# A load moved to another queue, two weight transfers cut into four, and some products moved ahead of scores, in a fused gated-attention and bilinear feed-forward kernel

## The chip, the cores and the metric

The kernel runs on one core of one Trainium2 chip. Its engines work side by side, each through its own list of instructions in order: TensorE (PE; its weight loads are shown as PEld), VectorE (DVE), ScalarE (ACT), GpSimd (POOL) and SyncE (SP). The metric is the device time of one launch in microseconds; less is better. A time is the median of several runs. The profile is that of one further execution.

## The reference

Four batches, eight heads, 768 positions, 48 numbers per head. A gated recurrence gives y, and y, with heads side by side (384 columns, 3072 tokens), goes through a bilinear feed-forward block.

```python
for t in range(S):
    state = alpha[:, :, t, :, None] * state + einsum('bhd,bhe->bhde', k[:, :, t], v[:, :, t])
    y[:, :, t] = einsum('bhd,bhde->bhe', q[:, :, t], state)
x = y.transpose(0, 2, 1, 3).reshape(B * S, H * D)
out = (x @ w_a) * (x @ w_b) @ w_out      # w_a, w_b: 384 x 1536, w_out: 1536 x 384
```

## The kernel before

**Chunks.** The work is cut into six chunks, 0 to 5, each of two batches (its halves u = 0 and 1) and 256 positions, two positions on each of 128 partitions. Chunks 0 and 1 hold the first 256 positions, 2 and 3 the next, 4 and 5 the last; the state goes on from 0 to 2 to 4 and from 1 to 3 to 5.

**The attention part of a chunk.** Alphas are loaded (a_t) and their logs taken on ScalarE (L420). Pairs of logs are added (L428; in later chunks L433 and L436, three instructions) and split into terms of lower precision (L474 and L482, or L497 twice), and TensorE sums them along the positions with a triangular matrix (L512 or L507). Exponentials of the sums (L541) scale keys and queries into QKp (L552); a query is first multiplied with a ratio (L519, L526), a key with an alpha (L526). QKp is turned into kqT: by TensorE and a copy (L593, L599, L601) in chunks 0 and 1, by a transposing DMA on SyncE's queue (L604) in chunks 2 to 5. Scores are products of kqT (L674), masked and moved out of PSUM by VectorE (L679) or by ScalarE and then VectorE (L683, L687). y is summed in PSUM from the carried state (L698, L703) and from scores and values (L698, L724). The copy of y out of PSUM (L764, L766) is xT in chunks 0 and 1; in later chunks it is ys, and a transposing DMA on SyncE's queue (L771) makes xT of it. The state is updated from L627 by L659 to L663.

**The feed-forward part.** The 1536 columns are 12 slices of 128. A product a or b of a slice is three matmuls (L786) over 256 tokens (one half of a chunk) or 512 (both). ScalarE moves a out of PSUM (L792, tiles as_, three buffers), VectorE multiplies it with b into prod (L800). When all 12 are there, an output of 128 tokens is 12 matmuls (L808), in two halves of six; it is moved out (L823, L825) and stored (L841). PSUM has eight banks of 512 columns; a bank can be written again when its reader is done.

**The order** is written out by hand, in a text called PROGRAM: each word is one operation, the number ahead of a line is the chunk, and the last letter of many names the engine (V, P for GpSimd, S, Y for SyncE). The text is run from top to bottom, so each engine's list is in the order of the text. Words that matter here: `ld` load, `W` a load of weight columns, `ln` the logs, `lx` or `l2` pair sums, `R`, `H` and `L` the splits, `A2`, `AQ` the sums, `ra` the ratio, `lv` the multiply with ratio or alpha, `mk`, `mq` the scaling into QKp, `T` the transposing DMA of QKp, `D` scores, `M`, `Mc`, `Mm` masking, `SA`, `SB`, `Y` the parts of y, `X` its copy and `XT` its transposing DMA, `K`, `KA`, `k` the state, `a f u i`, `b f u i` products of slice f into bank i (`*` for both halves), `as` and `pr` their way out, `o m h i` half h of output m, `ot`, `st` its way out. `gate...` is a copy of a single element on GpSimd: GpSimd goes on only when that element is written.

**The queues.** A load on GpSimd occupies that engine for 0.75 to 1.2 us while it is issued, and its queue serves one transfer behind the other. The weights, cast from float32 to bfloat16 on the way, come through GpSimd's queue, as do values, Wo and the loads of chunks 0 to 3 for the most part. SyncE's queue carries loads of later chunks, stores and the transposing DMAs, issued in the order of the text; each waits for its data before the next is issued. The alphas' tile a_t has two buffers, the tiles of logs and pair sums one.

In PROGRAM the load of chunk 4's alphas (`4: ld a * P`) stands among chunk 2's multiplies, ahead of `T 1` and `T 0` of chunk 2; that of chunk 5's (`5: ld a * Y`) stands behind chunk 2's `XT 0`.

Of the kernel before, what the change touches and what calls it, by code (L numbers as in the profile page):

```python
# [20 lines left out]
0: cm 1; ld v 1 P; c2 P; c3 P; D 0 1 5; M 0 1; D 0 0 0; SB 0 6; B 1a 4; Bs 1a; Mc 0 0; Mm 0 0 V; B 1b 5; Bs 1b; E 1a i; E 1a b; mq 1a V; mk 1a V; K 0 1 4; E 1b i  # L21
0: v 1 V; mk 1b V; E 1b b; mq 1b V; SA 0; Y 0; X 0 S; dk 1 0; C 1 0 3; Ce 1 0 V; k 0 1 V; b 1 0 6; W a 0 256; de 1; K 1 0 5; k 1 0 V
1: ld a 1 P
0: W a 256 768; W b 256 768
1: ld a 0 P
0: W a 768 1536; C 1 1 1; a 1 0 2; as 1 0; pr 1 0; Ce 1 1 V; W b 768 1536
1: ld q 0 P; ln 1
0: b 0 0 4; a 0 0 2; as 0 0; pr 0 0; D 1 0 6; D 1 1 0; M 1 1
1: ld k 0 P; l2 1 P; ld v 0 P; ld k 1 P
0: Mc 1 0; Mm 1 0 V  # L30
1: H 1 S
0: SB 1 1; a 2 0 3; a 5 0 6; a 3 0 7; as 3 0; a 4 0 4; as 4 0; as 5 0; b 4 0 0; b 3 0 7
1: L 1 V
0: pr 4 0; pr 3 0; SA 1; Y 1; X 1 V; b 2 0 0
1: A2 1 7; ld q 1 P
0: Wo 0 6
2: ld a * P
0: K 1 1 5
1: ln 0
0: as 2 0; pr 2 0  # L40
1: l2 0 V; E 1 b; E 1 i; H 0 S
0: a 3 1 4; a 5 1 2; k 1 1 V; as 3 1; b 3 1 0; a 4 1 1; b 5 0 7; pr 5 0; as 5 1; a 6 * 5; b 5 1 4; a 11 * 3; pr 5 1; pr 3 1; as 4 1; b 4 1 1; pr 4 1
1: L 0 V; dk * 6
0: Wo 6 12; as 11 *; as 6 *
1: ra 0
0: b 6 * 3; pr 6 *; b 11 * 0; pr 11 *
# [1 line left out]
1: lv 0 q P  # L48
2: ld q * P
1: ld v 1 P; lv 0 k V; mk 0 V  # L50
0: a 10 * 2; a 7 * 3
1: E 0 b; mq 0 V
0: as 10 *; a 2 1 4; as 2 1; b 10 * 1; pr 10 *; as 7 *; b 7 * 0; pr 7 *
1: v 0 S; ra 1
0: b 2 1 3; a 0 1 5
1: C 0 0 4
0: a 1 1 6; as 1 1
1: Ce 0 0 S
0: pr 2 1; b 1 1 1; pr 1 1; as 0 1
1: KA 0 02; k 0 0 V; k 0 1 V; C 0 1 7  # L60
0: b 0 1 6
1: Ce 0 1 S
2: ld k * P
1: lv 1 k P
0: pr 0 1
1: mk 1 V; lv 1 q P; mq 1 V
3: ld a * P
0: a 8 * 1; as 8 *; a 9 * 5; as 9 *
2: ld v * P
0: b 8 * 2; pr 8 *  # L70
1: D 0 0 6; M 0 0; D 0 1 3; Mc 0 1; SB 0 4
# [21 lines left out]
1: a 7 0 3; b 11 0 1; pr 11 0; KA 1 64; k 1 0 V; k 1 1 V; b 10 0 5; a 10 0 7; as 10 0; a 0 0 6  # L93
2: lv 0 k V
1: pr 10 0; b 0 0 1; a 3 0 4; as 0 0; pr 0 0
2: lv 1 k P; mk 1 V
1: as 3 0; b 3 0 7; a 1 0 6; as 1 0
4: ld a * P
1: b 7 0 0; b 1 0 4; pr 1 0; as 7 0; pr 7 0; pr 3 0
2: mk 0 V  # L100
1: SB 1 0
3: ln *
1: a 6 0 2; as 6 0; b 9 0 3; a 4 0 5; a 9 0 6; as 9 0; pr 9 0
2: mq 1 V; T 1
0: o 2 0 4
1: b 4 0 6; b 6 0 7
2: lv 0 q P; mq 0 V
1: pr 6 0
2: T 0
3: ld k * Y  # L110
# [15 lines left out]
1: pr 6 1  # L126
3: R 0
2: Mm 1 0 V
1: o 2 0 7
2: SB 1 3; D 0 1 1; Mc 0 1; Mm 0 1 V; k * 1 V  # L130
3: R 1
1: o 2 1 -; ot 2 S
0: st 2 Y
1: st 2 Y
2: D 0 0 5; Mc 0 0; Mm 0 0 V; gatem 0 0; SB 0 1; SA 1; Y 1; X 1 S; XT 1
3: lv 0 k P; lv 1 k P
1: a 4 1 7
4: ln *
1: as 4 1; b 9 1 0; pr 9 1; o 0 0 5
3: AQ 3  # L140
2: SA 0; Y 0; X 0 S; XT 0
5: ld a * Y
1: o 0 1 -; ot 0 V; a 1 1 6; a 10 1 1; as 1 1; as 10 1
3: E 0 b; E 0 i
1: b 4 1 2; pr 4 1; b 8 1 5; b 1 1 1; a 8 1 6; b 10 1 0; pr 1 1; o 3 0 2; pr 10 1; as 8 1; pr 8 1; o 3 1 -; ot 3 S; st 3 Y
2: a 4 * 7; as 4 *
3: E 1 b
2: a 5 * 6; b 4 * 3
3: E 1 i
1: st 0 Y  # L150
3: dr
4: lx V; R 0
3: mk 0 V; mq 0 V; T 0
4: ld q * Y
2: a 1 * 2; b 5 * 0; as 5 *; pr 5 *
4: ra 1
2: b 7 * 4; b 10 * 1; pr 4 *; a 10 * 6; as 10 *; pr 10 *
3: mk 1 V
2: a 7 * 0; b 1 * 5; a 0 * 6; b 0 * 7; as 1 *; as 7 *; pr 1 *; pr 7 *; as 0 *; a 3 * 0; b 9 * 1; pr 0 *
3: mq 1 V  # L160
# [5 lines left out]
3: KA * 06; D 0 0 4; M 0 0; dl; k * 0 V; k * 1 V  # L166
1: o 1 0 2
2: b 11 * 7
5: ln *
2: a 11 * 5; as 11 *; pr 11 *  # L170
1: o 1 1 -; ot 1 S
2: a 6 * 5; as 6 *; a 8 * 3; as 8 *
3: SB 0 6; D 0 1 0; M 0 1; T 1
4: ld k * Y
3: D 1 0 4; Mc 1 0
2: b 6 * 2; pr 6 *; b 8 * 3; pr 8 *
4: R 1
# [93 lines left out]
def kernel(  # L271
# [29 lines left out]
    ld = ctx.enter_context(tc.tile_pool(name="ld", bufs=2))  # L301
# [668 lines left out]
```

## Time and profile before

| | us |
|---|---|
| timed runs | 194.47, 194.94, 197.66 |
| median | 194.94 |
| profiled execution | 193.93 |
| its span, first to last instruction | 192.2 |
| granted TensorE clock | 0.999 |

A line of a group or timeline reads: start, duration, engine, line of the kernel, operation, what is written <- what is read, shapes, the number of instructions (x), and in brackets the idle time of that engine just before and what ended it. In the list of DMA issues the last number is the median time from issue to landing. A matmul's duration has a tail that runs beside the next one, so the cost of a further matmul is taken from the starts of two lines or from the chain. SyncE's lines (SPq) are the issuing of DMAs, not their transfer.

The DMA engines are busy from the start to about 115 us, and then in bursts (share of the 16 engines in 40 slices of the span, in tenths: 6999999999999999949993586998196005031013).

### The profile page before, as it was taken

The numbers are of one execution on the slowest core, as the hardware profiler recorded it, in microseconds if no ns is written. First come the engines' busy times: TensorE is split into PE (matmuls) and PEld (weight loads), VectorE is DVE, ScalarE is ACT, GpSimd is POOL, SyncE is SP. The second block draws the span as 40 slices with busy tenths as digits, with TensorE's granted clock in tenths as the row PEclk, the third lists the DMA queues.
The fourth block names the chain that finished last, engine by engine and source line by source line (L and its number), as shares of the span: only waits on it lengthen the run. The fifth ranks groups of instructions, "written<-read, shape, count | busy, mean of one in ns | idle before, by whom it ended". The sixth has DMA issues, their size and how long they took to land.

```text
span 192.2 us, 5878 instructions
## 1 busy us (share of the span) xinstructions
PE 184.1 (96%) x2509; PEld 111.3 (58%) x2509; DVE 136.1 (71%) x230; ACT 103.1 (54%) x189; POOL 50.1 (26%) x72
## 2 busy tenths in 40 slices
PE   7979799999999998999999999999999999999993
PEld 3567576766777875644556644555544565544562
DVE  4778767999899796688979499864953961156520
ACT  4385566887585567446566135875266521164301
POOL 8999746920641404000400020050000000000000
PEclk9999999999999999999999999999999999999999
DMA  6999999999999999949993586998196005031013
GB/s 149 246 216 215 243 241 254 249 245 261 252 233 219 191 213 248 215 126 229 151 220 54 141 185 154 160 173 111 47 198 144 3 3 123 3 108 56 2 41 123
DMA packets 67162, 30.96 MB, mean 161 GB/s; under 512 B 58064, under 2 KB 65120, under 8 KB 67136
## 3 DMA queue, kind: packets, MB, share of 16 engines
q0 software_dynamic: 18640, 14.16, 41.9%
q1 hardware_dynamic: 48352, 16.34, 40.6%
q8 instruction: 19, 0.31, 0.7%
q10 hardware_dynamic: 144, 0.10, 0.2%
q14 instruction: 7, 0.06, 0.1%
HBM read 25.98 MB, written 4.74 MB: 160 GB/s over the span
## 4 chain that ended last, share of the span: by engine, by line
PE 86%; POOL 6%; DMA 4%; issue 1%; DVE 0%; ACT 0%; POOLq 0%; DVEq 0%
PE psum L786 48%; PE psum L808 24%; DMA wb_t<-in_moe_w_b_dram 4%; PE psum L674 3%; PE psum L724 2%; PE psum L627 2%; PE psum L698 2%; PE psum L703 1%; PE psum L507 1%; PE psum L819 1%; POOL v_t L413 1%; PE psum L593 1%; POOL a_t L413 1%; POOL wa_t L393 1%; POOL k_t L413 0%
## 5 line engine op out<-in xcount | busy, mean ns | idle before, releaser
L786 PE MATMUL psum<-xT,wb_t 128*128 128x512 bf16 (+1 forms) x270 | 57.0, 337 | 0.6 <-DMA wb_t<-in_moe_w_b_dram 0.5
L786 PE MATMUL psum<-xT,wa_t 128*128 128x512 bf16 (+1 forms) x270 | 56.1, 337 | 1.1 <-issue 0.7
L808 PE MATMUL psum<-wo_t,prod 128*128 128x384 bf16 x276 | 48.5, 326 | 0.0
L786 PEld LDWEIGHTS <-wb_t 128*128 128x128 bf16 x270 | 25.5, 98 | 21.1 <-DMA wb_t<-in_moe_w_b_dram 0.8
L786 PEld LDWEIGHTS <-wa_t 128*128 128x128 bf16 x270 | 25.6, 98 | 20.8 <-issue 1.0
L808 PEld LDWEIGHTS <-prod 128*128 128x128 bf16 x276 | 26.1, 98 | 16.9
L683 ACT ACTIVATE m<-psum 128x1024 bf16<-128x1024 f32 x16 | 16.3, 1023 | 6.5 <-PE psum L674 6.3
L825 DVE COPY ot<-psum 128x384 f32<-128x384 f32 (+1 forms) x13 | 6.9, 539 | 15.9 <-PE psum L808 13.4
L526 POOL TENSOR_TENSOR q_t<-q_t,ra 128x384 f32<-128x384 f32 x8 | 8.7, 1084 | 34.3 <-DMA q_t<-in_q_dram 17.3
L823 ACT ACTIVATE ot<-psum 128x384 f32<-128x384 f32 (+1 forms) x12 | 5.7, 477 | 12.9 <-PE psum L808 11.9
L420 ACT ACTIVATE la<-a_t 128x1536 f32<-128x1536 f32 (+2 forms) x9 | 9.5, 1057 | 3.4 <-DMA a_t<-in_alpha_dram 3.4
L687 DVE TENSOR_TENSOR m<-m,mask 128x1024 bf16<-128x1024 bf16 x16 | 10.8, 685 | 0.3 <-ACT m L683 0.3
L679 DVE TENSOR_TENSOR m<-psum,mask 128x1024 bf16<-128x1024 f32 x8 | 9.8, 1222 | 1.7 <-PE psum L674 1.5
L526 POOL TENSOR_TENSOR k_t<-k_t,a_t 128x384 f32<-128x384 f32 x5 | 5.3, 1064 | 19.0 <-DVE QKp L552 17.5
L552 DVE TENSOR_TENSOR QKp<-k_t,invb 128x768 bf16<-128x768 f32 x10 | 9.9, 992 | 0.2
L552 DVE TENSOR_TENSOR QKp<-q_t,beta 128x768 bf16<-128x768 f32 x10 | 9.3, 949 | 0.0
L674 PE MATMUL psum<-kqT 64*64 64x128 bf16 x384 | 8.6, 218 | 0.5 <-DVE prod L800 0.2
L413 POOL DMA_DIRECT2D v_t<-in_v_dram x8 | 8.6, 1070 | 0.5 <-issue 0.4
L674 PEld LDWEIGHTS <-kqT 64*64 64x64 bf16 x384 | 6.3, 107 | 3.2 <-issue 2.1
L764 ACT ACTIVATE ys<-psum 128x768 bf16<-128x768 f32 x7 | 5.6, 809 | 4.3 <-PE psum L703 2.3
L413 POOL DMA_DIRECT2D a_t<-in_alpha_dram x6 | 6.3, 1042 | 4.0 <-DMA wa_t<-in_moe_w_a_dram 2.2
L446 PE MATMUL psum<-wz 128*128 128x512 bf16 x17 | 5.5, 472 | 1.2 <-DVE og L338 1.2
(273 smaller groups left out, 270.9 us busy)
## 6 DMA issues: line engine op xcount, KB each, us to landing
out_dram<-ot SPq DMA_DIRECT2D x23, 192.0 KB, 2.2
a_t<-in_alpha_dram POOLq DMA_DIRECT2D x3, 768.0 KB, 14.5
k_t<-in_k_dram SPq DMA_DIRECT2D x3, 768.0 KB, 7.2
q_t<-in_q_dram POOLq DMA_DIRECT2D x2, 768.0 KB, 13.0
v_t<-in_v_dram POOLq DMA_DIRECT2D x4, 384.0 KB, 10.1
q_t<-in_q_dram SPq DMA_DIRECT2D x2, 768.0 KB, 6.6
a_t<-in_alpha_dram POOLq DMA_DIRECT2D x3, 384.0 KB, 5.6
q_t<-in_q_dram POOLq DMA_DIRECT2D x3, 384.0 KB, 13.4
```

What stands on the lines that cost most here:

```text
L413: eng.dma_start(out=t[:, us, hs].rearrange("p b h r d -> p (b h) (r d)"), in_=src[ch.b0 + us.start:ch.b0 + us.stop, hs, ch.s * 2 * C:(ch.s ...
L420: nc.scalar.activation(out=ch.la[:, us, hs].rearrange("p b h r d -> p (b h r d)"), in_=ch.a[:, us, hs].rearrange("p b h r d -> p (b h r d) ...
L526: eng.tensor_mul(x, x, by)
L552: eng.tensor_mul(QKp[ch.c % 2][:, u, j, :, hs, :D], src[:, u, hs].rearrange("p h r d -> p r h d"), f)
L674: nc.tensor.matmul(s2[g * HC:(g + 1) * HC, r, p, rk, :], lhsT=ch.kqT[u][rs, 1, rk, 2 * h + p, g * HC:(g + 1) * HC], rhs=queriesT(ch, u, 2 ...
L679: nc.vector.tensor_mul(m.rearrange("p r a k s -> p (r a) (k s)"), ch.s2[u, h].rearrange("p r a k s -> p (r a) (k s)"), maskn(4))
L683: nc.scalar.activation(out=m.rearrange("p r a k s -> p (r a) (k s)"), in_=ch.s2[u, h].rearrange("p r a k s -> p (r a) (k s)"), func=AF.Copy)
L687: eng.tensor_mul(x, x, maskn(4))
L786: nc.tensor.matmul(p, lhsT=(wa_t, wb_t)[w][:, kk, f * 128:(f + 1) * 128], rhs=ch.xT[:, us.start // 2:us.stop // 2, kk].rearrange("p u g s ...
L808: nc.tensor.matmul(op, lhsT=ch.prod[:, f, at:at + C], rhs=wo_t[:, f, :], start=(f == 0), stop=(f == NFF - 1))
L823: nc.scalar.activation(out=o_, in_=i_, func=AF.Copy)
L825: eng.tensor_copy(o_, i_)
```

## The change

Only PROGRAM and one new gate are changed.

- The weights' columns 256 to 768 come as four transfers instead of two: a 256 to 512, b 256 to 512, a 512 to 768, b 512 to 768. Six products of slices 2 to 5 for chunk 0's first half are put in that order, with those of a and b taking turns; b of slices 2 and 3 now stand ahead of chunk 0's second y. Some banks change.
- A product of both halves (`a 10 *`) stands ahead of `b 6 *`, and `a 1 1` of chunk 0 ahead of chunk 1's first turning (`C 0 0`).
- Chunk 4's alphas are loaded by SyncE behind chunk 2's `XT 0`, in the place of chunk 5's, and those by SyncE behind chunk 4's keys. Logs, pair sums and splits of both chunks move back with them: chunk 4's `ln` and a ratio behind ScalarE's eviction of chunk 2's second slice (`as 5 *`), its `lx` behind `pr 4 *`, its first split behind chunk 3's output half.
- In chunk 2, `mq 1` and `T 1` stand ahead of `mk 0`; a gate lets GpSimd multiply the other half's queries only when `mk 1` has written.
- `a 4 1` and the output half `o 0 0` of chunk 1 stand ahead of chunk 2's last scores (`D 0 0`), `o 0 1` ahead of chunk 2's last y (`Y 0`).

```diff
-0: W a 256 768; W b 256 768
+0: W a 256 512; W b 256 512; W a 512 768; W b 512 768
...
-0: SB 1 1; a 2 0 3; a 5 0 6; a 3 0 7; as 3 0; a 4 0 4; as 4 0; as 5 0; b 4 0 0; b 3 0 7
-1: L 1 V
-0: pr 4 0; pr 3 0; SA 1; Y 1; X 1 V; b 2 0 0
+0: a 2 0 4; as 2 0; a 3 0 5; as 3 0; b 2 0 6; pr 2 0; b 3 0 0; a 4 0 7; as 4 0; a 5 0 1; as 5 0; pr 3 0
+1: H 1 S; L 1 V
+0: SA 1; Y 1; X 1 V; b 4 0 4; pr 4 0; b 5 0 5; pr 5 0
...
-2: lv 1 k P; mk 1 V
+2: lv 1 k P; mk 1 V; gatek 1; lv 0 q P
 1: as 3 0; b 3 0 7; a 1 0 6; as 1 0
-4: ld a * P
 1: b 7 0 0; b 1 0 4; pr 1 0; as 7 0; pr 7 0; pr 3 0
-2: mk 0 V
+2: mq 1 V; T 1
...
-2: mq 1 V; T 1
+2: mk 0 V
...
-2: D 0 0 5; Mc 0 0; Mm 0 0 V; gatem 0 0; SB 0 1; SA 1; Y 1; X 1 S; XT 1
+1: a 4 1 5; as 4 1; o 0 0 7
+2: D 0 0 1; Mc 0 0; Mm 0 0 V; gatem 0 0; SB 0 5; SA 1; Y 1; X 1 S; XT 1
 3: lv 0 k P; lv 1 k P
-1: a 4 1 7
-4: ln *
-1: as 4 1; b 9 1 0; pr 9 1; o 0 0 5
+1: o 0 1 -; ot 0 V
 3: AQ 3
+1: b 9 1 0; pr 9 1
 2: SA 0; Y 0; X 0 S; XT 0
-5: ld a * Y
+4: ld a * Y
...
+    def gate_k(x, u):
+
+        nc.gpsimd.tensor_copy(go, QKp[x.c % 2][0:1, int(u), 1, 0, 0, 0:1])
```

More of the change, by code (lines that the diff above doesn't have):

```diff
@@ L27 @@
 1: ld q 0 P; ln 1
-0: b 0 0 4; a 0 0 2; as 0 0; pr 0 0; D 1 0 6; D 1 1 0; M 1 1
+0: b 0 0 4; a 0 0 2; as 0 0; pr 0 0; D 1 0 6; SB 1 2; D 1 1 0; M 1 1
 1: ld k 0 P; l2 1 P; ld v 0 P; ld k 1 P
 0: Mc 1 0; Mm 1 0 V
-1: H 1 S
-0: SB 1 1; a 2 0 3; a 5 0 6; a 3 0 7; as 3 0; a 4 0 4; as 4 0; as 5 0; b 4 0 0; b 3 0 7
-1: L 1 V
-0: pr 4 0; pr 3 0; SA 1; Y 1; X 1 V; b 2 0 0
+0: a 2 0 4; as 2 0; a 3 0 5; as 3 0; b 2 0 6; pr 2 0; b 3 0 0; a 4 0 7; as 4 0; a 5 0 1; as 5 0; pr 3 0
+1: H 1 S; L 1 V
+0: SA 1; Y 1; X 1 V; b 4 0 4; pr 4 0; b 5 0 5; pr 5 0
 1: A2 1 7; ld q 1 P
@@ L37 @@
 2: ld a * P
-0: K 1 1 5
+0: K 1 1 6
 1: ln 0
-0: as 2 0; pr 2 0
 1: l2 0 V; E 1 b; E 1 i; H 0 S
-0: a 3 1 4; a 5 1 2; k 1 1 V; as 3 1; b 3 1 0; a 4 1 1; b 5 0 7; pr 5 0; as 5 1; a 6 * 5; b 5 1 4; a 11 * 3; pr 5 1; pr 3 1; as 4 1; b 4 1 1; pr 4 1
-1: L 0 V; dk * 6
+0: a 3 1 1; a 5 1 2; k 1 1 V; as 3 1; b 3 1 0; a 4 1 3; as 5 1; b 5 1 4; as 4 1; b 4 1 5; pr 3 1; pr 5 1; a 6 * 6; a 11 * 7; pr 4 1
+1: L 0 V; dk * 1
+0: a 10 * 2
 0: Wo 6 12; as 11 *; as 6 *
@@ L50 @@
 1: ld v 1 P; lv 0 k V; mk 0 V
-0: a 10 * 2; a 7 * 3
+0: a 7 * 4
 1: E 0 b; mq 0 V
-0: as 10 *; a 2 1 4; as 2 1; b 10 * 1; pr 10 *; as 7 *; b 7 * 0; pr 7 *
+0: as 10 *; a 2 1 5; as 2 1; b 10 * 1; as 7 *; b 7 * 0; pr 7 *; pr 10 *
 1: v 0 S; ra 1
-0: b 2 1 3; a 0 1 5
-1: C 0 0 4
-0: a 1 1 6; as 1 1
+0: b 2 1 3; a 0 1 6; a 1 1 4
+1: C 0 0 5
+0: as 1 1
 1: Ce 0 0 S
-0: pr 2 1; b 1 1 1; pr 1 1; as 0 1
-1: KA 0 02; k 0 0 V; k 0 1 V; C 0 1 7
-0: b 0 1 6
+0: pr 2 1; b 1 1 7; pr 1 1; as 0 1
+1: KA 0 02; k 0 0 V; k 0 1 V; C 0 1 1
+0: b 0 1 4
 1: Ce 0 1 S
@@ L67 @@
 3: ld a * P
-0: a 8 * 1; as 8 *; a 9 * 5; as 9 *
+0: a 8 * 7; as 8 *; a 9 * 5; as 9 *
 2: ld v * P
@@ L103 @@
 1: a 6 0 2; as 6 0; b 9 0 3; a 4 0 5; a 9 0 6; as 9 0; pr 9 0
-2: mq 1 V; T 1
+2: mk 0 V
 0: o 2 0 4
 1: b 4 0 6; b 6 0 7
-2: lv 0 q P; mq 0 V
+2: mq 0 V
 1: pr 6 0
@@ L128 @@
 2: Mm 1 0 V
-1: o 2 0 7
+1: o 2 0 6
 2: SB 1 3; D 0 1 1; Mc 0 1; Mm 0 1 V; k * 1 V
@@ L134 @@
 1: st 2 Y
-2: D 0 0 5; Mc 0 0; Mm 0 0 V; gatem 0 0; SB 0 1; SA 1; Y 1; X 1 S; XT 1
+1: a 4 1 5; as 4 1; o 0 0 7
+2: D 0 0 1; Mc 0 0; Mm 0 0 V; gatem 0 0; SB 0 5; SA 1; Y 1; X 1 S; XT 1
 3: lv 0 k P; lv 1 k P
-1: a 4 1 7
-4: ln *
-1: as 4 1; b 9 1 0; pr 9 1; o 0 0 5
+1: o 0 1 -; ot 0 V
 3: AQ 3
+1: b 9 1 0; pr 9 1
 2: SA 0; Y 0; X 0 S; XT 0
-5: ld a * Y
-1: o 0 1 -; ot 0 V; a 1 1 6; a 10 1 1; as 1 1; as 10 1
+4: ld a * Y
+1: a 1 1 1; a 10 1 2; as 1 1; as 10 1
 3: E 0 b; E 0 i
-1: b 4 1 2; pr 4 1; b 8 1 5; b 1 1 1; a 8 1 6; b 10 1 0; pr 1 1; o 3 0 2; pr 10 1; as 8 1; pr 8 1; o 3 1 -; ot 3 S; st 3 Y
+1: b 4 1 7; pr 4 1; b 8 1 0; b 1 1 5; a 8 1 6; b 10 1 1; pr 1 1; o 3 0 2; pr 10 1; as 8 1; pr 8 1; o 3 1 -; ot 3 S; st 3 Y
 2: a 4 * 7; as 4 *
@@ L151 @@
 3: dr
-4: lx V; R 0
 3: mk 0 V; mq 0 V; T 0
@@ L155 @@
 2: a 1 * 2; b 5 * 0; as 5 *; pr 5 *
-4: ra 1
-2: b 7 * 4; b 10 * 1; pr 4 *; a 10 * 6; as 10 *; pr 10 *
+4: ln *; ra 1
+2: b 7 * 4; b 10 * 1; pr 4 *
+4: lx V
+2: a 10 * 6; as 10 *; pr 10 *
 3: mk 1 V
@@ L168 @@
 2: b 11 * 7
-5: ln *
 2: a 11 * 5; as 11 *; pr 11 *
@@ L172 @@
 2: a 6 * 5; as 6 *; a 8 * 3; as 8 *
+4: R 0
 3: SB 0 6; D 0 1 0; M 0 1; T 1
 4: ld k * Y
+5: ld a * Y
 3: D 1 0 4; Mc 1 0
@@ L196 @@
 4: mq 0 V; mk 0 V
-5: lx V
+5: ln *; lx V
 3: a 9 * 3; a 0 * 2; a 8 * 6; b 11 * 7; as 9 *; as 11 *; as 0 *; pr 11 *; b 9 * 2; b 0 * 1; pr 9 *
@@ L867 @@
         "gatet": gate_t,
+        "gatek": gate_k,
         "gatem": gate_m,
```

## The prediction

> **What bounds the kernel now.** I read the page first, then TensorE's waits, then the chain of waits in order of time, then each engine's timeline around the places where TensorE stands still. From the page, the span, the busy shares and the chain's shares:
>
> ```profile
> span 192.2 us, 5878 instructions
> PE 184.1 (96%) x2509; PEld 111.3 (58%) x2509; DVE 136.1 (71%) x230; ACT 103.1 (54%) x189; POOL 50.1 (26%) x72
> ...
> PE 86%; POOL 6%; DMA 4%; issue 1%; DVE 0%; ACT 0%; POOLq 0%; DVEq 0%
> ```
>
> TensorE is the bound: 86% of the chain. What a change of order can win is the time in which TensorE stands idle, and the chain shows where that is (start, us, what; an "issue" piece is idle time without a waiter):
>
> ```profile
> 14.42 8.19 DMA wb_t<-in_moe_w_b_dram
> ...
> 23.48 0.95 PE psum L698 x54
> ...
> 74.52 0.51 PE psum L724 x32
> ...
> 76.32 0.72 issue
> ...
> 79.30 1.95 PE psum L808 x12
> ```
>
> TensorE's own timeline has the rest, the wait for weights at 20 to 23 us; and its weight loads (PEld) have one wait at 66 us, which the list of waits puts on VectorE but which a transposing DMA ends:
>
> ```profile
> 20.67 1.48 PE L786 MATMUL psum<-xT,wa_t 128*128 128x256 bf16 x12 [0.39 <-DMA wa_t<-in_moe_w_a_dram]
> 22.65 0.83 PE L786 MATMUL psum<-xT,wb_t 128*128 128x256 bf16 x6 [0.50 <-DMA wb_t<-in_moe_w_b_dram]
> ...
> 25.51 0.83 PE L786 MATMUL psum<-xT,wa_t 128*128 128x256 bf16 x6
> ```
> ```profile
> 66.12 0.48 PEld L674 LDWEIGHTS <-kqT 64*64 64x64 bf16 x32 [0.50 <-DMA kqT<-QKp]
> ```
>
> After 23 us the idle time is thus 0.50 + 0.72 = 1.2 us of 192. Everything that follows is about single microseconds, against the 3.9 us that are 2%, about what a measurement of this kernel can tell from no change.
>
> **Part 1, the weights in four transfers.** Before, weight columns 256 to 768 come as two transfers of 384 KB, the first landing at 20.6, the second at 22.61. After, four of 192 KB. If a half costs half, they land near 19.5, 20.5, 21.6 and 22.6. Before, TensorE has only the four a-products of slices 2 to 5 to do until 22.65; b of 2, 3 and 4 and the second half of chunk 0's y (23.48, 0.95) follow. A product of three 256-column matmuls costs (1.48 - 0.83) / 2 = 0.33, from the rows with twelve and with six. After, b of 2 and 3 and that y run before the last quarter lands; only b of 4 and 5 wait for it. Step by step: b of 2 by 21.0 (its bank is free when ScalarE has read the scores), b of 3 at 21.4 (the bank is masked until then), a of 4 and 5 by 22.4, y by 23.35, b of 4 and 5 by 24.0, chunk 1's sums and state 24.0 to 24.7, then the products that start at 25.51 now, with b of slice 5 (0.33) already done: 25.51 - 24.75 + 0.33 = about 1.1 us in hand.
>
> That time does not reach the end. Chunk 1's first keys come through the same queue behind all weights, and VectorE's chain hangs on them:
>
> ```profile
> 32.61 0.56 DVE L526 TENSOR_TENSOR k_t<-k_t,a_t 128x384 f32<-128x384 f32 x1 [0.31 <-DMA k_t<-in_k_dram]
> ...
> 34.15 0.95 DVE L552 TENSOR_TENSOR QKp<-q_t,beta 128x768 bf16<-128x768 f32 x1
> ...
> 46.75 0.96 DVE L497 TENSOR_TENSOR ll<-lh 128x768 f32<-128x768 f32 x1
> ```
> ```profile
> 35.26 0.61 PE L593 MATMUL psum<-ident,QKp 128*128 128x128 bf16 x8
> 35.71 0.49 PE L786 MATMUL psum<-xT,wa_t 128*128 128x256 bf16 x3
> ...
> 47.88 0.36 PE L507 MATMUL psum<-l,utb 64*64 64x384 bf16 x4
> ```
>
> The multiply of the queries ends at 35.10 and TensorE turns them at 35.26. The changed order has put one more product (a of slice 1, the row at 35.71, 0.33) ahead of this turning; so at 35.2 the lead is 0.33 and at most 0.1 more, and the rest of the 1.1 goes into a wait. VectorE is then busy almost without a gap to 47.71, 0.17 before chunk 2's sums on TensorE. So this part is worth **0.35 us**, as long as the keys land at the same time.
>
> Do halves cost half? The nearest rows are issue times and issue-to-landing times of transfers that follow one another in that queue:
>
> ```profile
> 15.18 0.89 POOL L413 DMA_DIRECT2D a_t<-in_alpha_dram  x1
> ...
> 18.42 0.90 POOL L413 DMA_DIRECT2D k_t<-in_k_dram  x1
> ...
> 20.27 0.92 POOL L413 DMA_DIRECT2D v_t<-in_v_dram  x1
> ```
> ```profile
> a_t<-in_alpha_dram POOLq DMA_DIRECT2D x1, 384.0 KB, 8.7
> ```
> ```profile
> k_t<-in_k_dram POOLq DMA_DIRECT2D x1, 384.0 KB, 14.1
> ```
> ```profile
> v_t<-in_v_dram POOLq DMA_DIRECT2D x1, 192.0 KB, 13.2
> ```
>
> Two more issues hold GpSimd for at most 0.9 us each. The loads behind them don't feel it: they lie 8.7 to 14 us in the queue. A pair sum of chunk 1 behind them on GpSimd comes up to 1.8 us later; with its split on ScalarE and VectorE it reaches TensorE about when that asks for it, at 24.0. Were it 0.3 late, the wait for the keys would hide it.
>
> Alphas of 384 KB land at 23.9, 1.3 us behind the weights at 22.6; values of 192 KB land at 33.5, 1.0 behind the keys at 32.5. Read as a fixed part, that is 2 x 1.0 - 1.3 = 0.7 us in each transfer, and two more transfers would put the keys 1.4 us later. Read as the values' short rows (they are cast on the way), it says nothing of weights, whose rows stay long. At the other end, nothing is lost. I take 0, since the queue is never empty here and transfers overlap, and keep 1.4 for the range. The Trainium skill (DMA: Bandwidth & Descriptors, Rules for kernel authors and the table of measured sizes) speaks against the split: it wants DMAs of 1 MiB or more, and gives 0.95 us for 64 KB and 6.15 us for 1 MB. An estimate from that line is 0.6 us of fixed cost per transfer, 1.2 us for the two; by it the result would be that of the second rival below.
>
> **Part 2, chunk 4's alphas leave GpSimd's queue.** The stall at 66 us is for the transpose of chunk 2's second half:
>
> ```profile
> 59.03 7.19 SPq L604 DMA_TRANSPOSE kqT<-QKp  x2
> ...
> 77.30 0.45 SPq L413 DMA_DIRECT2D a_t<-in_alpha_dram  x1
> ...
> 84.56 2.02 SPq L604 DMA_TRANSPOSE kqT<-QKp  x1
> ```
> ```profile
> 54.70 1.19 POOL L413 DMA_DIRECT2D a_t<-in_alpha_dram  x1 [1.89 <-DVE prod L800]
> ```
> ```profile
> 58.02 1.81 DVE L552 TENSOR_TENSOR QKp<-q_t,beta 128x768 bf16<-128x768 f32 x2
> ```
>
> Two such transposes take 7.19 us there, one alone 2.02. The alphas' 768 KB, issued at 54.70, run beside them. Gone from there, they leave the transposes bounded by 2 to 3.6 us each. Besides, VectorE now multiplies the second half's queries ahead of the first half's keys, so the first transpose is issued near 57.3 instead of 59.03. Even at the slow pace it lands 1.7 us sooner, which is more than 0.50 plus the 0.35 of lead. The new wait on GpSimd (for the scaled keys of that half, done near 55.5) holds a query multiply that starts at 55.9 now; nothing is lost. **0.5 us** won, so 0.85 in hand at the last scores of chunk 2's second half.
>
> **Part 3, long products earlier.** A product and half an output go ahead of chunk 2's last scores, the other half ahead of its last y. TensorE's work is the same; y's second half ends 1.0 us of work later. Its cover shrinks: until chunk 2's first product there are then seven products of 0.33 and one output of 1.95, 4.2 us, against the copy and the transpose:
>
> ```profile
> 75.06 0.81 ACT L764 ACTIVATE ys<-psum 128x768 bf16<-128x768 f32 x1 [0.35 <-PE psum L724]
> ```
> ```profile
> 73.09 4.02 SPq L771 DMA_TRANSPOSE xT<-ys  x2
> ```
>
> The second of the two follows the copy at 75.87 and is issued by 77.11, 1.2 later. When it lands, no row tells; within 3 us of its start, the path is 3.9 us and the cover holds by 0.3, and at the 7.19 / 2 = 3.6 of the transposes above 0.3 is lost. The gap of 0.72 at 76.32 has no waiter but TensorE itself. The profile counts 0.31 MB on the instruction queue. The Trainium skill (Runtime: NRT & Kernel Launch, Instruction fetch mechanics) says that instructions come in blocks of 16 KiB while the block before executes, mostly hidden; by it a block came late here, and with fewer bytes in flight it need not. With the gap gone the lead is 1.6 us at chunk 2's first product, with the gap kept 0.85.
>
> **Part 4, what is late next.** Chunk 4's alphas are now issued where chunk 5's were, behind the last y transpose. That y ends at 75.03 - 0.85 + 0.97 (half an output) = 75.15; copy and transpose issue bring the load to 77.4. Its price:
>
> ```profile
> a_t<-in_alpha_dram SPq DMA_DIRECT2D x1, 768.0 KB, 6.4
> ...
> k_t<-in_k_dram SPq DMA_DIRECT2D x3, 768.0 KB, 7.2
> ```
>
> They land at 83.8. The log (1.48) and a ratio (0.55) now stand in ScalarE's queue ahead of the evictions, so the next eviction ends at 86.4, and TensorE's product that needs its bank goes at 86.4 instead of 87.56: lead at most 1.2. On VectorE the pair sums wait for the log (85.3) and take 0.55 + 1.12:
>
> ```profile
> 80.64 1.12 DVE L436 TENSOR_TENSOR l<-la 64x384 f32<-64x384 f32 x2
> ...
> 87.09 0.73 DVE L800 TENSOR_TENSOR prod<-as__1828,psum 128x512 bf16<-128x512 bf16 x1 [1.16 <-ACT as__1828 L792]
> ...
> 92.27 0.73 DVE L800 TENSOR_TENSOR prod<-as__1870,psum 128x512 bf16<-128x512 bf16 x1 [0.28 <-ACT as__1870 L792]
> ...
> 97.19 0.72 DVE L800 TENSOR_TENSOR prod<-as__1989,psum 128x512 bf16<-128x512 bf16 x1
> ```
> ```profile
> 92.79 1.48 ACT L420 ACTIVATE la<-a_t 128x1536 f32<-128x1536 f32 x1
> ```
> ```profile
> 83.64 0.55 ACT L519 ACTIVATE ra<-la 128x384 f32<-128x384 f32 x1
> ```
> ```profile
> 98.41 0.24 PE psum L703 x16
> ```
>
> So the product of 87.09 starts at 86.95, and VectorE goes on as now, 0.12 earlier, without the gap of 0.28 (TensorE is ahead): the product of 97.19 ends at 97.5 instead of 97.91. It frees the bank into which TensorE starts chunk 3's y (98.34): there the lead is 98.34 - 97.55 = **0.8 us**. No other TensorE wait is in the trace behind this, and chunk 5's alphas, behind chunk 4's keys on the same queue, land by 94.4 + 2 x 7.2 = 109 at the latest, before the pair sums at 112. The sum is -0.8 us, whether or not the 0.72 gap goes.
>
> **The rivals.** *More is won*: chunk 4's alphas land a microsecond sooner, VectorE never binds, and the whole 1.6 us arrives. For it: 5 to 6 us would do, little else is in flight at 78. Against: 6.4 was measured at this very place. 192.3 for the profiled execution.
>
> *Small transfers cost*: chunk 1's keys land 1.4 us later, VectorE's chain to 47.7 with them; the 0.35 becomes -1.05, and all that follows, chunk 4's alphas included, shifts by 1.4: 193.93 - 0.8 + 1.4 = 194.5. For it: the values' row. Against: a queue that is never empty. The Trainium skill's rule on size (DMA: Bandwidth & Descriptors) would make this case the likely one.
>
> *The alphas come too late, and it is slower*: the log stands before eight evictions in ScalarE's queue, the pair sums before seven products in VectorE's, and TensorE waits for their banks. Each microsecond past 6.4 costs one; at 7.2, the keys' row, nothing is left; at 9 it is 193.93 - 0.8 + 2.6 = 195.7; over 2% from 11 us. For it: the load shares the engines with stores and chunk 3's values, which took 11 us beside the keys. Against: these values are issued 11 us earlier.
>
> *It doesn't do what it says*: transposes stay slow for another reason, the stall at 66 stays; 0.35 remains, 193.6.
>
> **How the numbers follow.** The sum stands against the profiled execution, 193.93 us (span 192.2). Timed runs are 194.47, 194.94 and 197.66; I take 194.5 as the level of this kernel, between the profiled one and the median, and so predict 194.5 - 0.8 = 193.7. Chances: the forecast 0.42 (with the stall kept at 66, 0.08 more), more won 0.20, small transfers cost 0.15, late alphas 0.15 (of it 0.04 over 2%). Forecast and rivals lie at 192.9 to 196.3 on that level; the half microsecond between runs of one kernel goes on both sides, and the slow end is cut where 2 in 10 are left: 192.3 to 195.6. Faster by over 2% needs 3.9 us, more than all idle time named here: 0.01. Slower by over 2%: 0.04 from late alphas and 0.01 from what I do not see. Within 2%: 0.94.
>
> **What would show it.** Right: TensorE's wait for weights splits, with b-products before 22; the turning near 35.2 waits on VectorE by about half a microsecond; no wait on the transposes at 65; the log of chunk 4 ends near 85.3; TensorE waits on ScalarE near 86 and on VectorE near 97. Wrong: keys landing past 33.5; the log past 86.5; chunk 2's first product waiting for the transposed y; a new gap without a waiter in chunk 3's scores, where chunk 5's alphas are now in flight.

## The result, and the profile after

| | before | after |
|---|---|---|
| median of 17 runs each, us | 194.62 | 196.35 |
| lowest and highest, us | 193.96, 197.66 | 195.06, 199.76 |
| profiled execution, us | 193.93 | 195.28 |
| its span, us | 192.2 | 193.5 |

The ratio after to before is 1.0083, with a 95% interval of 1.0062 to 1.0104. That is within 2%, but it is a loss, and 196.35 lies outside the range of 192.3 to 195.6. Disturbed runs, such as the highest of each, are left out of all ratios here.

From the page of the changed kernel, the span, the busy shares, the instruction queue (packets, MB, share of the DMA engines) and the chain's shares:

```profile
span 193.5 us, 5882 instructions
PE 185.3 (96%) x2509; PEld 112.1 (58%) x2509; DVE 134.9 (70%) x230; ACT 103.3 (53%) x189; POOL 50.0 (26%) x74
...
q8 instruction: 19, 0.31, 0.7%
...
PE 91%; DVE 4%; issue 2%; ACT 1%; DVEq 0%
```

TensorE still binds, 91% of the chain. The pieces of weights have left the chain (4% before), and "issue", idle time without a releaser, has doubled. Where it is, the list of TensorE's waits says (line waited for, total us, times, longest):

```profile
PE psum L724 <- issue: 2.4, 1, 2.4
PE psum L446 <- DVE og L338: 1.2, 1, 1.2
PE psum L627 <- ACT prod L541: 0.6, 1, 0.6
```

The two behind the first are from the start of the kernel and stood there before too (1.2 and 0.8), and every further one is 0.2 or less: there is no wait for weights left, none for transposes, and no 0.7 in chunk 2's products. One idle stretch of 2.4 us has come instead, in a y (L724). The chain of waits gives the places (start, us, what):

```profile
36.56 0.61 PE psum L593 x8
...
47.67 0.63 PE psum L507 x12
...
65.63 0.57 PE psum L674 x32
...
80.07 11.65 PE psum L786 x54
...
97.31 0.24 PE psum L703 x16
...
103.31 0.38 PE psum L724 x22
103.69 2.36 issue
106.05 0.30 PE psum L724 x10
106.35 5.96 PE psum L808 x36
```

The same chain of the kernel before, at the same work:

```profile
47.95 0.63 PE psum L507 x12
...
66.14 0.63 PE psum L674 x32
...
81.25 11.65 PE psum L786 x54
...
98.41 0.24 PE psum L703 x16
...
104.42 0.51 PE psum L724 x32
104.92 5.96 PE psum L808 x36
```

Read side by side, the changed kernel leads by 47.95 - 47.67 = 0.28 us at chunk 2's sums, 0.51 at its last scores, 1.18 at its first product and 1.10 when chunk 3's y starts. In this profile it does what it was predicted to do up to 103 us, and a little more; a second profile, below, has a smaller lead. Then TensorE stands still in the middle of chunk 3's second y, 22 of 32 matmuls done, and at the output behind it the lead of 1.10 has become a lag of 106.35 - 104.92 = 1.43. Both kernels then take the same time to the end.

What stands around this gap on SyncE and ScalarE (start, duration, engine, line; in brackets the idle time before and what ended it):

```profile
93.14 1.09 SPq L413 DMA_DIRECT2D k_t<-in_k_dram  x1
94.33 3.33 SPq L413 DMA_DIRECT2D a_t<-in_alpha_dram  x1
101.73 7.07 SPq L771 DMA_TRANSPOSE xT<-ys  x2
```
```profile
106.94 1.48 ACT L420 ACTIVATE la<-a_t 128x1536 f32<-128x1536 f32 x1 [1.69 <-DMA a_t<-in_alpha_dram]
```

Chunk 5's alphas, 768 KB, are now issued at 94.33 behind chunk 4's keys, and land about 106.9. Nothing in this y reads them. But they are in flight all through the stretch in which the gap comes. Busy times by window (us, then each engine's busy time and count, the granted clock, the packets' time as a share of the DMA engines, which can exceed 1, and the GB/s), before and then after:

```profile
99.00:103.00 4.00, 4.00 (x103) 2.42 (x96) 4.00 (x6) 2.85 (x4) 0.00 (x0) 1.00 0.97 88
```
```profile
99.00:103.00 4.00, 4.00 (x106) 2.48 (x108) 4.00 (x8) 1.80 (x3) 0.00 (x0) 1.00 1.34 242
```

88 GB/s have become 242 in the four microseconds ahead of the gap; the clock is 1.00 in both.

### What the gap is: a late block of instructions

The trace has 2509 matmuls and as many weight loads, 5018 instructions of TensorE, and the instruction queue moves 0.31 MB in 19 packets, some 264 instructions to a packet. Counted along the trace, the gap in the changed kernel stands ahead of instruction 3263 = 12 x 256 + 191, and the 0.72 of the kernel before ahead of 2493 = 9 x 256 + 189. (Instructions that only wait are not counted, so a place is good to two or three; the float32 matmuls of the start stand twice in the trace, which moves every place behind 31 us by the same number.) So I took both gaps for a block of 256 that was not there in time. If a border lies every 256 instructions at this remainder, the 5018 hold 19 borders, as many as there are packets. The instruction packet of the DMA records shows the one at the gap; from 99.4 to 103.2 us the changed kernel moves none, and from 103.2 to 104.7 this one (packets, MB, share of 16 engines; 5.2% of 16 x 1.5 us is 1.25 us):

```profile
q8 instruction: 1, 0.02, 5.2%
```

Put beside each other, with the packet's start from the DMA records and the two instructions located by counting:

| profile of | block before entered (instruction 3007) | packet starts | delay | instruction 3263 starts | packet start to it | gap |
|---|---|---|---|---|---|---|
| before | 100.56 | 101.14 | 0.58 | 104.64 | no wait | none |
| after | 99.46 | 103.31 | 3.85 | 106.05 | 2.74 | 2.36 |

Before, the packet starts 0.6 us after TensorE enters the block ahead of it, and TensorE reaches the new block 3.50 us behind the packet's start, without a wait. After, the packet starts 3.85 us late, and TensorE goes on 2.74 us behind it. The block between takes 103.69 - 99.46 = 4.2 us, because it holds y, scores and sums, the shortest instructions of the kernel; so a delay of 4.2 - 2.7 = 1.5 us is free and the rest is a gap: 3.85 - 1.5 = 2.35. That comes out by construction here, since both terms are of this trace; the other runs test it.

### The profile page after: what moved, and what is told of

Same layout as the page of the kernel before. It is cut to its first block, busy times and chain, and to the rows that moved or that the text cites. A ratio compares the mean times of both kernels' runs of the same rounds, so it can differ in the third digit from the quotient of the medians.

```text
span 193.5 us, 5882 instructions
## 1 busy us (share of the span) xinstructions
PE 185.3 (96%) x2509; PEld 112.1 (58%) x2509; DVE 134.9 (70%) x230; ACT 103.3 (53%) x189; POOL 50.0 (26%) x74
## 4 chain that ended last, share of the span: by engine, by line
PE 91%; DVE 4%; issue 2%; ACT 1%; DVEq 0%
PE psum L786 48%; PE psum L808 24%; PE psum L674 3%; PE psum L698 2%; PE psum L627 2%; PE psum L724 2%; PE psum L446 2%; PE psum L593 2%; PE psum L462 2%; PE psum L703 1%; PE psum L507 1%; DVE QKp L552 1%; PE psum L819 1%; PE psum L573 1%; DVE prod L800 1%
## 5 line engine op out<-in xcount | busy, mean ns | idle before, releaser
L526 POOL TENSOR_TENSOR q_t<-q_t,ra 128x384 f32<-128x384 f32 x8 | 8.2, 1025 | 33.3 <-DMA q_t<-in_q_dram 17.6
L724 PE MATMUL psum<-v_t,m 64*128 64x48 bf16 x256 | 4.6, 180 | 2.4 <-issue 2.4
```

What stands on the lines that cost most here:

```text
L526: eng.tensor_mul(x, x, by)
L724: nc.tensor.matmul(y[:, g, h * D:(h + 1) * D], lhsT=ch.m[u, h // 4][gs, h % 2, h // 2 % 2, rk, :], rhs=value(ch, gs, u, rk, h), start=not ...
```

## The experiments

The theory: a block's fetch is delayed by the transfers in flight when it is asked for; the moved load of chunk 5's alphas made chunk 3's crowded. The rivals: the gap is a wait for data that the profile doesn't show; or the loss is that of the small weight transfers, and the gap a symptom. Every median below stands against runs of the kernel before on the same chip.

### Chunk 5's alphas later

```diff
-5: ld a * Y
 ...
-5: ld k * Y
+5: ld k * Y; ld a * Y
 ...
-5: ln *; lx V
 ...
+5: ln *; lx V; lv 0 k V
```

The logs, pair sums and first multiply of chunk 5 were moved back with the load, ahead of chunk 4's `K * 0 2`, and its first split behind that.

> The changed kernel with one thing more: chunk 5's alphas are issued behind chunk 5's keys (near 108 us) instead of behind chunk 4's (94.3), and chunk 5's logs, pair sums, one key multiply and first split stand some 10 us later. Theory (late instruction block): the 2.36 us gap without a waiter in chunk 3's last y is the wait for TensorE's next block of instructions, whose fetch stands behind chunk 5's alphas; without them there the gap is under 0.5 us and the time is 193.0 to 194.0, about 1 us below the kernel before. Rival (the y transposes hold the fetch): the transpose of the other half is issued at 101.7 as before, the gap stays at 1 us or more and the time at 195.5 or more.

Measured: 196.25 us, ratio 1.0081 (1.0051 to 1.0110). The gap at the same instruction fell to 0.59, a little over the 0.5 that was forecast, and the time missed the 193.0 to 194.0 altogether: TensorE lost as much at another place, which the list of waits shows:

```profile
PE psum L784 <- DVE prod L798: 2.0, 2, 1.9
PE psum L722 <- issue: 0.6, 1, 0.6
```

The pair sums that this edit had to move stand in front of products on VectorE at 126 us. The run speaks for the theory at the gap, and its time says nothing on the loss.

### The kernel before with one more load

The kernel before, with a load of 768 KB into a tile that nobody reads, on SyncE's queue behind chunk 4's keys, where the change put chunk 5's alphas.

```diff
+5: decoy Y
 ...
```

> The kernel before, plus one load of 768 KB of alphas into a tile that nobody reads, on SyncE's queue behind chunk 4's keys. Theory: TensorE gets a gap without a waiter of 1 to 3 us in chunk 3's last y, between 103 and 107 us, and the kernel is that much slower than before (195.5 to 197.5). Rival (the gap comes of another part of the change, such as the order of products or the turned queues): no gap over 0.5 us there, time within 0.5 us of before.

Measured: 196.38 us, ratio 1.0091 (1.0061 to 1.0121), as large a loss as the change's with none of its other parts. The chain at the place:

```profile
104.84 0.38 PE psum L730 x21
105.22 1.51 issue
106.73 0.30 PE psum L730 x11
```

The gap is in the same y (line numbers are six higher in this kernel), ahead of instruction 3261; the gap at 77 us is there too, ahead of 2493, and 3261 - 2493 = 768 is 3 x 256. No instruction waits for this load, so a hidden wait for its data is ruled out: a load in flight is enough.

### The borders of the blocks shifted

The changed kernel with its warming matmuls in smaller pieces, 102 instructions more at the start; the warming results are not used.

```diff
-fill 7 2
+warm 28 2
 ...
-fill 9 2
+warm 36 2
 ...
-fill 1 1
+warm 4 1
```

> The changed kernel with the 17 warming matmuls of 512 columns at the start replaced by 68 of 128 columns, 102 more rows in TensorE's list at the same columns of work; the DMAs are untouched. Theory: blocks of 256 rows begin 102 rows earlier in the program, so the gap moves from the last y of chunk 3 to the output products or sums ahead of it (row 3002 of the changed kernel's list), and is 1 to 3.5 us long; the time stays within 1 us of the changed kernel. Rival (TensorE waits there for data or a bank that the trace does not name): the gap stays in the same y, after 22 of its 32 matmuls, at about 2.4 us.

Measured: 196.34 us, 1.0074 (1.0043 to 1.0105). In the list of waits:

```profile
PE psum L808 <- issue: 1.5, 1, 1.5
...
PE psum L674 <- issue: 1.0, 1, 1.0
PE psum L724 <- issue: 0.3, 1, 0.3
```

The gap has left the y for the output products 102 instructions earlier, and is again ahead of instruction 3263 of the list; the two others stand ahead of 2239 = 8 x 256 + 191 and 4029 = 15 x 256 + 189. The place goes with the count, not with the work.

### The weights' part alone

The changed PROGRAM up to `3: ld a * P`, the rest as before. In a first run the seam put a product into a bank that was not yet free; the second run gives it another.

```diff
-a 8 * 1
+a 8 * 7
```

> The first third of the change alone: four weight transfers and the order of chunk 0 and 1 as changed, everything from the load of chunk 3's alphas on as before. Theory: 0.2 to 0.4 us faster than before up to 48 us, then the wait for the transpose at 66 us takes it back or not; time 0.0 to 0.4 us below before (194.2 to 194.6), no gap over 1 us in chunk 3's y. Rival (halved transfers put the keys later and make the loss): 0.5 to 1.5 us slower than before.

> As the run with the first third of the change alone, with one bank put right at the seam: a product of slice 8 goes to bank 7 as in the changed kernel, where the first mix made it wait 1.1 us for a copy that reads bank 1. Theory: that wait goes, 0.9 to 1.3 us faster than the first mix, so 194.1 to 194.6, level with before. Rival (the split itself loses by late keys): 0.5 us or more above before, with the turning at 35 us waiting 0.4 us or more.

Measured: 195.37 us, 1.0031 (1.0007 to 1.0055), above the 194.2 to 194.6 expected, with the seam's wait and a gap at a border (1.24, ahead of instruction 2239); with the other bank 194.25 us, 0.9967 (0.9944 to 0.9991). From the waits of the first and of the second:

```profile
PE psum L702 <- issue: 1.2, 1, 1.2
PE psum L785 <- ACT kqT L598: 1.1, 1, 1.1
```
```profile
PE psum L785 <- ACT as__1735 L791: 0.6, 1, 0.6
```

So the transfers in four and the new order, together, win 0.33%, the lowest median of this study; what the split alone costs, this run does not separate. The wait that is left stands ahead of instruction 2495 = 9 x 256 + 191, where the kernel before has its 0.72; the profile puts it down to ScalarE, but the packet for that block starts at 74.73 against 74.85 before, so I read it as the same gap.

### Fewer bytes at the border: three runs

Each moves one load of the changed kernel out of the crowded stretch: chunk 5's alphas behind chunk 3's first y transpose; chunk 4's values behind a gate until its keys are multiplied; and, in the third, the first move on the late part of the change alone, with the weights as before.

```diff
-5: ld a * Y
 ...
 3: SB 1 4; D 1 1 0; Mc 1 1; Mm 1 1 V; SA 0; Y 0; X 0 S; XT 0
+5: ld a * Y
```
```diff
-4: lv 0 q P; ld v * P
+4: lv 0 q P
 ...
-4: E 1 i; E 1 b; mk 1 V
+4: E 1 i; E 1 b; mk 1 V; gatek 1; ld v * P
```

> The changed kernel with chunk 5's alphas issued behind the first transpose of chunk 3's y (near 103.7) instead of behind chunk 4's keys (94.3); nothing else moves. Theory: the block of instructions that is asked for at about 99.7 is fetched before these alphas start; the gap in chunk 3's last y is under 0.6 us, the time 193.3 to 194.3, 2 us below the changed kernel. Rival (keys and values of chunk 4 and the transpose are enough to delay the fetch): gap over 1 us, time 195 or more. Second risk: the other y transpose runs beside the alphas and lands late; then TensorE waits at the first product of chunk 3, near 111, by up to 1.5 us.

> The changed kernel with chunk 4's values (384 KB, GpSimd's queue) issued only when chunk 4's first keys are scaled, near 107, instead of at 92.9; chunk 5's alphas stay behind chunk 4's keys. Theory (late block by the sum of the bytes in flight): keys and alphas alone are through near 101 to 102, the gap falls to 0 to 1.2 us, the time to 194 to 195.3. Rival (the alphas alone, on SyncE's queue, delay the fetch whatever else flows): the gap stays at 1.8 us or more.

> The kernel before up to the load of chunk 3's alphas (two weight transfers, its order of products), and from there the changed kernel with chunk 5's alphas behind the first transpose of chunk 3's y. Theory: the transposes at 66 us are waited for no longer and the gap at 76 goes; 1.0 to 1.5 us faster than before, 193.2 to 193.7, and within 0.4 us of the same version with the weights in four. Rival (the first third carries the gain): no faster than before.

| | median | ratio to before | gap at the border |
|---|---|---|---|
| alphas moved | 194.66 | 0.9977 (0.9948 to 1.0006) | 0.81 |
| values moved | 194.82 | 0.9986 (0.9965 to 1.0006) | 0.96 |
| late part, alphas moved | 195.00 | 1.0014 (0.9988 to 1.0040) | 0.84 |

Each shrinks the gap to some 0.8 to 1.0, and the loss is gone with it. Chunk 5's alphas are thus not special: moving chunk 4's values does as well. No run is clearly faster than before, though. The first missed its forecast of time (193.3 to 194.3) and of the gap (under 0.6), the second met both, and the third, forecast 1.0 to 1.5 us faster, came out as its rival had it: no faster than before.

### Both loads moved

> The changed kernel with both loads moved that the two runs before moved one at a time: chunk 5's alphas go behind the first transpose of chunk 3's y, and chunk 4's values wait on GpSimd until its keys have been multiplied. Theory (the block of TensorE's instructions that begins in chunk 3's second y, near 103.5 us, is fetched late because of all the bytes in flight): each move alone left 0.8 to 1.0 us of the 2.4, so both together leave under 0.5 us, the profiled span is 191.8 to 192.6 us and the median 193.7 to 194.6, ratio 0.995 to 1.000. Rival (the gap has a floor of its own at this place, whatever is in flight, and each move reached it): 0.8 us or more stays and the time is that of either run, 194.7 to 194.8. Second rival (the values, later by some microseconds, become the wait of chunk 4's first scores or products): a new wait on VectorE or GpSimd behind 115 us, and 195 us or more.

Measured: no gap at the border, and a packet that starts at 100.72, 0.8 us after TensorE enters the block before it, in a window with hardly a transfer:

```profile
99.00:103.00 4.00, 4.00 (x101) 2.35 (x100) 4.00 (x7) 2.28 (x3) 0.00 (x0) 1.00 0.12 24
```

The time did not follow: 195.09 us, 1.0033 (1.0010 to 1.0055), with a profiled execution of 194.22; the forecast was 193.7 to 194.6. Of what the border gave back, a new wait at 110.75, ahead of the first product of chunk 3, takes half a microsecond; the profile names VectorE there, in the second profile below the transposed y, which is what this product reads:

```profile
110.75 1.47 PE L786 MATMUL psum<-xT,wa_t 128*128 128x512 bf16 x6 [0.50 <-DVE QKp L552]
```

With the alphas alone moved it was 0.19 already, since their load runs beside that transpose. So the forecast of the gap came true and that of the total did not.

### Both kernels profiled again

The medians of the changed kernel and of the last one lie 1.1 and 0.9 us above their profiled executions; a second profile of each, unedited, looks for the difference.

> The changed kernel, unedited, profiled a second time. Its profiled execution took 195.28 us, while the median of its runs is 196.35. Theory (a block of TensorE's instructions is fetched late, and how late hangs on what else is in flight, so it varies from run to run): the span again has a gap without a releaser at the second y of chunk 3, at the same instruction, but of another length, 1.5 to 4 us, and the span minus this gap is within 0.5 us of 193.5 - 2.4 = 191.1 us. Rival (the runs differ by something spread over the whole span, such as the clock): the gap is again 2.2 to 2.5 us, and the rest of the span differs.

> The kernel in which both loads were moved, unedited, profiled a second time. Its profiled execution took 194.22 us with no gap without a releaser in chunk 3's second y, while the median of its runs is 195.09. Theory: a gap of 0.3 to 1.5 us without a releaser shows this time at a start of a block, there or at another, and explains the time above 194.22. Rival: no such gap, and the time above 194.22 lies elsewhere.

Measured: 196.12 and 196.16 us, both near their medians. The chain of the changed kernel, second profile:

```profile
37.29 0.61 PE psum L593 x8
...
98.02 0.24 PE psum L703 x16
...
104.40 2.46 issue
106.86 0.29 PE psum L724 x10
```

The gap is 2.46 against 2.36, as the rival had it: in these two profiles the length does not vary. Of the difference of 0.8 us, 0.7 is there at 37.29 already (36.56 in the first profile): chunk 1's first keys were multiplied at 33.49 instead of 32.76. So when chunk 3's y starts, this run leads the kernel before by 98.41 - 98.02 = 0.39 us, not by 1.10, and its time is the nearer to the median. In the other kernel the gap stays away, and the time above its first profile is also lost at the start; its first row of the windows has a granted clock of 0.87 against 1.00, and TensorE waits 1.3 us at chunk 1's first turning, whose keys are multiplied at 34.77 (32.81 in the first profile):

```profile
0.00:15.00 15.00, 12.35 (x116) 7.72 (x117) 7.88 (x18) 7.02 (x12) 13.69 (x35) 0.87 1.05 199
```
```profile
PE psum L593 <- DVE QKp L552: 1.3, 1, 1.3
```

What spreads the runs of one kernel lies, in these two pairs, in the first 37 us. Whether that explains the whole of the 195.09 is not shown.

### The borders moved, every load left in place

Again only the warming matmuls are cut smaller (119 instead of 17, the results unused): 204 more instructions, so that each border falls 52 instructions further on in the work and no block from 25 to 175 us is shorter than 5.7 us.

```diff
+    def wee(n, i):
+        for _ in range(n):
+            nc.tensor.matmul(bank(i)[:C // 2, :C // 2], lhsT=wz[:, :C // 2], rhs=wz[:, :C // 2], start=True, stop=True)
 ...
-fill 7 2
+wee 42 2; warm 7 2
 ...
-fill 9 2
+wee 54 2; warm 9 2
 ...
-fill 1 1
+wee 6 1; warm 1 1
```

> The changed kernel with all its loads where the change put them; only the matmuls that warm TensorE before its first data come in smaller pieces (119 instead of 17, with as many columns in all), so that TensorE's list is 204 instructions longer there and every border of 256 falls 52 instructions further on in the work. Counted against the trace of the changed kernel, the block that now takes 4.2 us (from the end of chunk 3's scores to its second y) then takes 6.8 us, and no block between 25 and 175 us takes less than 5.7. Theory (a fetch is asked for when the block before it begins, starts up to 3.9 us later beside transfers, and takes 2.7 us from its start to the first instruction: in all 6.6 us): no gap over 0.5 us without a releaser behind 25 us, 2.4 us less than the changed kernel, a span of 191.0 to 191.8 and a median of 193.6 to 194.6, ratio 0.994 to 1.000, unless the longer list at the start costs it there. Rival (the gap belongs to these matmuls or to the loads beside them, wherever the borders lie): a gap of 1.5 us or more in chunk 3's scores, y or output, and a median above 195.5.

Measured: 194.88 us, 0.9997 (0.9976 to 1.0018): 1.5 us less than the changed kernel with the same loads at the same places. The window is nearly as full as after the change (197 GB/s against 242), and chunk 3's second y runs through:

```profile
99.00:103.00 4.00, 4.00 (x139) 2.45 (x138) 3.81 (x5) 3.00 (x5) 0.00 (x0) 1.00 1.60 197
```
```profile
105.38 0.51 PE psum L728 x32
105.89 5.96 PE psum L812 x36
```

The block's packet even starts at 105.21, 3.4 us after TensorE enters the block before it at 101.84, and it does not matter, since that block lasts 6.6. The median lies above the forecast of 193.6 to 194.6; one reason is in the list of waits:

```profile
PE psum L790 <- DMA xT<-ys: 1.3, 1, 1.3
```

It is chunk 2's first product at 82.04, which waits for the transposed y: 4.7 us from the transpose's issue (77.30), where the changed kernel issues it at 76.60 (its two transposes stand from 73.81 to 78.33 on SyncE, the second for 1.73) and goes on at 80.07, 3.5 later, without a wait. Why it took longer here was not tried.

### All together at this border

TensorE enters the block ahead of this border between 99.46 and 102.18 us, so a window from 99 to 103 us is not the same work in every run. Here the GB/s are those of the 3.5 us from that entry on; the rows for before and after are

```profile
100.56:104.06 3.50, 3.50 (x104) 2.35 (x104) 3.50 (x7) 1.72 (x2) 0.00 (x0) 1.00 0.23 23
```
```profile
99.46:102.96 3.50, 3.50 (x104) 2.35 (x104) 3.50 (x7) 1.73 (x2) 0.00 (x0) 1.00 1.33 248
```

| profile of | GB/s, 3.5 us from the entry | delay of the packet | delay - 1.5 | gap |
|---|---|---|---|---|
| both loads moved | 6 | 0.78 | none | none |
| both loads moved, again | 6 | 1.29 | none | none |
| weights alone | 16 | 1.27 | none | none |
| before | 23 | 0.58 | none | none |
| weights alone, other bank | 25 | 0.75 | none | none |
| chunk 5's alphas later | 126 | 2.36 | 0.86 | 0.59 |
| alphas moved | 162 | 2.53 | 1.03 | 0.81 |
| late part, alphas moved | 173 | 2.46 | 0.96 | 0.84 |
| values moved | 201 | 2.66 | 1.16 | 0.96 |
| before and one more load | 240 | 3.11 | 1.61 | 1.51 |
| after, again | 247 | 3.89 | 2.39 | 2.46 |
| after | 248 | 3.85 | 2.35 | 2.36 |

The delay gives the gap to some 0.3 us. Counted this way the delay grows with the bytes moved in that time. They are not the whole of it: with the borders moved, 261 GB/s go with 3.4 us, and at another border of the changed kernel, entered at 66.19, 324 GB/s go with 2.2. What else sets the length was not tried.

## Why the prediction was wrong

**The step that failed** stands in Part 4: "No other TensorE wait is in the trace behind this, and chunk 5's alphas, behind chunk 4's keys on the same queue, land by 94.4 + 2 x 7.2 = 109 at the latest, before the pair sums at 112." The arithmetic held (they land near 106.9), and the conclusion did not: the load was priced only at when its data is there, hence at nothing. Its price was 2.36 us of TensorE, paid by an instruction block that came late beside it. One extra load at this place makes such a gap (1.51) and such a loss in the kernel before; this load moved on takes 1.55 of the 2.36 away; and the borders moved, with every load left in place, take the gap away altogether, which shows by which way the load acts. The text had named "a new gap without a waiter in chunk 3's scores, where chunk 5's alphas are now in flight" as a sign of being wrong, but gave it neither a price nor a chance, so that no rival ends there. A gap of this kind, 0.72 long, was in the trace of before; it was treated only as something that could go, while the change moved 768 KB into a stretch that stood at 88 GB/s.

**Part 1, the weights.** Right in kind: the wait for weights is gone, the gain is cut off by chunk 1's keys, and 0.28 us reach chunk 2's sums in the first profile where 0.35 was forecast. That halves cost nothing was the value taken, and it was probably too low. In the three profiles with two transfers (before, one more load, late part) the keys are multiplied at 32.61 to 32.75 us; in the eleven with four, at 32.48 to 34.77, the middle one at 33.17. That points to some 0.4 us for the split there; three profiles against eleven, with a wide spread, don't settle the size. The first profile of the changed kernel, at 32.76, is one of the early ones, so a part of its lead is luck. The 1.2 us that the prediction estimated for the two transfers more from the Trainium skill's sizes (DMA: Bandwidth & Descriptors, the table of measured sizes) is three times the difference seen.

**Part 2, the transposes.** Right: no wait for them is left; the first is issued at 57.31 as forecast, and the two take 6.20 instead of 7.19. The term was too large: 0.50 is the idle time of the weight loads, and the lead at that place grew only from 0.28 to 0.51, so TensorE itself had lost some 0.2.

**Part 3, the long products.** Right, and the better of its two cases: the 0.72 gap is gone and the lead at chunk 2's first product is 1.18. The explanation by fewer bytes fits: from 71 to 75 us 247 GB/s were moved before and 110 after, and the packet for the block started 3.6 us after TensorE entered the block before it, and 0.8.

```profile
71.00:75.00 4.00, 4.00 (x153) 3.04 (x146) 3.50 (x6) 3.71 (x5) 0.75 (x2) 1.00 1.60 247
```
```profile
71.00:75.00 4.00, 4.00 (x118) 2.39 (x119) 3.22 (x6) 1.88 (x3) 1.05 (x2) 1.00 0.82 110
```

The cover of y's transpose, given as 0.3 us thin, held in the changed kernel and failed by 1.3 in the last experiment.

**Part 4, chunk 4's alphas.** The logs end at 85.2 where 85.3 was forecast, but that is luck: two errors cancel. The load is issued at 78.50 instead of 77.4, and its data is there 5.2 us later instead of 6.4, when the logs start:

```profile
78.50 0.46 SPq L413 DMA_DIRECT2D a_t<-in_alpha_dram  x1
```
```profile
83.70 1.48 ACT L420 ACTIVATE la<-a_t 128x1536 f32<-128x1536 f32 x1 [1.09 <-DMA a_t<-in_alpha_dram]
```

That VectorE would bind at 97 was too careful for the first profile: the lead there is 1.10, not 0.8.

So the parts that the prediction costed bring 1.1 us by 98 us in the first profile, more than the 0.8 forecast, but 0.4 in the second; and the one it costed at nothing takes 2.4 to 2.5. In the four other profiles with the same order up to 92 us (alphas moved, values moved, and the two with both moved), chunk 3's y starts at 97.35, 98.31, 97.71 and 99.71, against 98.34 before and 97.24 and 97.95 in the two of the changed kernel. A gain of 0.8 is thus not shown for a usual run, and no version with the whole change, with the gap or without it, came to the 193.7 that was forecast: the lowest median is 194.66, with the alphas moved. The late block explains the loss; the late keys and the new waits explain some of what is missing beyond it, and how much is open.

## What to carry to other kernels

Where TensorE stands still with no releaser, count its instructions: if such places lie a multiple of 256 apart and an instruction packet starts shortly ahead of them, suspect a late block. Here it was cured by moving bytes or by moving the border. Before a load is moved, look not only at when its data must be there, but at what else goes through the DMA engines then, instruction blocks included; a block of short matmuls (here 4.2 us for 256 instructions) has little to spare. A gain read from one profile is worth a second one: here 1.1 us became 0.4. An order tuned by hand is tuned to its borders too: a few instructions more or less at the start shift them all.

## What the runs showed of the hardware

TensorE's instructions come in packets of 256: 19 for 5018 instructions, 20 for 5120 and for 5222. At the border studied a packet starts 0.6 to 1.3 us after TensorE enters the block before it beside 6 to 25 GB/s, and 2.4 to 3.9 us after it beside 126 to 248 GB/s; from its start to the first instruction behind the wait it takes 2.5 to 2.8 us at this border (2.2 at the one of the kernel before, at 77 us). The entry is not quite the moment of the request: behind long products, at the last border, a packet started 2.3 us ahead of it (169.35 against 171.61 in the trace of after). The Trainium skill (Runtime: NRT & Kernel Launch, Instruction fetch mechanics) has such blocks of 256, fetched while the block before executes, and calls the cost of crossing a border mostly hidden. The traces agree on the blocks; hidden it is only where the block before lasts longer than delay and fetch, and here it cost up to 2.46 us at one border.
